# Seven plain value blocks in layer 0 of a four-layer kernel, and attention outputs repacked through DRAM from 512 to 448 rows ahead of the output projection

## The chip, the cores and the metric

One core of a Trainium2 chip. The time is the device time of one execution in microseconds (us). The kernel before takes 396.25 us (median of 3, 396.03 to 396.76). Most executions agree within 1%. Profiles show one execution each, on the same core; their span starts at the first instruction and is some 1.7 us shorter than the timed run.

## The reference

Four layers, A, B, A, B, each `x = x + layer(layernorm(x))`, on 2048 tokens of width 448, bf16.

```python
def _A_ref(x, wqkv, wo):              # H = 16 heads of 28, window W = 8, dilation 2
    q, k, v = ...                     # x @ wqkv, split by head
    idx = pos[:, None] - arange(W) * 2          # each token sees itself and 7 earlier ones, 2 apart
    logits = einsum("bhsd,bhswd->bhsw", q, kg) * 28 ** -0.5   # masked where idx < 0
    o = einsum("bhsw,bhswd->bhsd", softmax(logits), vg)
    return o.reshape(B, S, D) @ wo
def _B_ref(x, w_gate, w_up, w_down):  # F = 1792
    return ((x @ w_gate) * (x @ w_up)) @ w_down
```

## The kernel before

The program states operations with estimated durations, dependencies and priorities; a list scheduler in the program turns them into one fixed order for each engine, and semaphores carry the dependencies. All is unrolled. Tokens go through attention in value blocks of 120 queries; most attention operations serve a pair of blocks. The output projection works on double blocks of 256 tokens, 8 of them in each of the layers 0 and 2.

A head has 28 values; it sits in 32 rows, so that four heads fill the 128 partitions. The normalised attention `oT` is therefore 4 x 128 = 512 rows, 64 of which are padding, and the projection reads it as it stands, 8 chunks of 64 rows against weights with zeros in the padding:

```python
oT = sb([128, 4, HALF], bf, "oT")
...  # normalisation, VectorE, key ("N", li, qb)
tensor_tensor(oT[:, :, a % HALF:...], O, R_sb, ALU.mult)
...
def y_blocks(li, B, prio):
    twin_blocks(lambda w: ps[:, bk[w], 0:D],
                lambda w, c, lo: oT[lo:lo + 64, c, 128 * ((B + w) % 8):...],
                lambda w, c, lo: wo_g[lo:lo + 64, c, :], ..., [range(4)], ..., nd + WO, prio, bk)
```

For values, twelve heads are multiplied out by TensorE (336 columns). The last four ride in the padding rows of the query/key weights and reach their place over DRAM (`vt`), by 7 stores per chunk and a transposed load per block. The first three blocks of layer 0 (`PLAIN = 3`) skip that and multiply out all 448 columns. Loads and stores are issued by the Sync engine (SP) in the program's fixed order; what stands ahead holds up what is ready (4.3 us for the stores of one double block in the changed kernel's trace, below).

## Time and profile before

| | before |
|---|---|
| time | 396.25 us |
| TensorE (PE) busy | 98% of the span |
| PE in the chain that ended last | 88% |
| PE waiting, from 57.8 to 376 us | 2.3 us |

The prediction below shows the page's main lines. Two more things matter for what follows. The waits of PE (line waited for, total us, times, longest), the longest and the one at the end:

```profile
PE ps L877 <- issue: 1.8, 1, 1.8
...
PE ps L985 <- DVE hT L973: 0.9, 1, 0.9
```

The whole list has six entries, and no DMA is among them. "issue" means that PE stood still with nothing in the profile to wait for. And two stretches that the prediction left out (columns: stretch, length, busy time of PE, weight loads, VectorE, ScalarE, GpSimd, then PE clock, DMA share, GB/s):

```profile
57.80:143.00 85.20, 85.00 (x1398) 47.98 (x1398) 70.03 (x155) 45.28 (x92) 0.00 (x0) 1.00 0.29 48
143.00:245.00 102.00, 101.69 (x1664) 57.06 (x1662) 75.37 (x161) 49.92 (x97) 0.00 (x0) 1.00 0.22 37
```

PE loses 0.2 us in the first and 0.3 us in the second.

### The profile page before, as it was taken

How to read it: one execution, taken by the hardware profiler on the slowest of the kernel's cores; microseconds unless marked ns; L12 is line 12 of the kernel's file. 1: busy time of each engine (PE TensorE's matmuls, PEld its weight loads, DVE VectorE, ACT ScalarE, POOL GpSimd, SP SyncE). 2: the span in 40 equal slices, each digit the busy share in tenths (PEclk: the TensorE clock that was granted, in tenths of full speed). 3: DMA queues.
4: the chain of work that ended last, by engine and by line, in shares of the span. 5: the costliest groups of instructions: out<-in, count | busy, mean ns of one | idle time of the engine just before them, and what ended most of it. 6: DMA issues, size and time to landing. Idle time of an engine off the chain costs nothing.

```text
span 396.3 us, 13913 instructions
## 1 busy us (share of the span) xinstructions
PE 386.9 (98%) x6142; PEld 217.3 (55%) x6142; DVE 279.8 (71%) x604; ACT 199.4 (50%) x387; POOL 10.0 (3%) x38
## 2 busy tenths in 40 slices
PE   8999999999999999999999999899999999999996
PEld 5645468555445455545556677554545444544584
DVE  6997899988957857785679656695693867344152
ACT  5779895647514556345643445653661354043040
POOL 7200000000000000000000000000000000000000
PEclk9999999999999999999999999899999999999999
DMA  8992153532021412031020354008002120400000
GB/s 270 289 285 60 26 67 62 61 75 53 2 49 28 75 17 54 7 54 20 11 49 3 54 76 73 3 8 124 20 2 48 58 40 0 79 18 2 24 27 23
DMA packets 54107, 22.71 MB, mean 57 GB/s; under 512 B 44992, under 2 KB 53120, under 8 KB 54048
## 3 DMA queue, kind: packets, MB, share of 16 engines
q1 hardware_dynamic: 53136, 19.72, 25.4%
q10 hardware_dynamic: 912, 2.12, 1.9%
q8 instruction: 48, 0.79, 0.9%
q14 instruction: 11, 0.09, 0.1%
HBM read 8.54 MB, written 2.83 MB: 29 GB/s over the span
## 4 chain that ended last, share of the span: by engine, by line
PE 88%; DVE 6%; ACT 2%; issue 2%; DMA 1%; DVEq 0%
PE ps L964 42%; PE ps L698 25%; PE ps L682 15%; PE ps L877 2%; PE ps L843 2%; PE ps L985 1%; DVE st L614 1%; DVE x_sb L935 1%; DVE xn_sb L635 1%; DMA x_sb<-in_A_x_dram 1%; DVE E_sb L860 1%; PE ps L644 1%; DVE qk L734 1%; ACT qk L734 0%; DVE R_sb L905 0%
## 5 line engine op out<-in xcount | busy, mean ns | idle before, releaser
L964 PE MATMUL ps<-xnTb,WGU 64*128 64x512 bf16 (+1 forms) x1960 | 181.3, 336 | 0.6 <-ACT qk L734 0.4
L964 PEld LDWEIGHTS ps<-xnTb,WGU 64*128 64x128 bf16 x1960 | 95.1, 95 | 73.2 <-DVE x_sb L935 0.7
L970 ACT ACTIVATE g_sb<-ps 128x512 bf16<-128x512 f32 (+1 forms) x140 | 71.4, 513 | 121.7 <-PE ps L964 120.4
L973 DVE TENSOR_TENSOR hT<-g_sb,ps 128x512 bf16<-128x512 bf16 (+1 forms) x140 | 78.8, 573 | 42.3 <-ACT g_sb L970 38.8
L698 PE MATMUL ps<-WD,hT 64*128 64x448 bf16 x840 | 83.3, 349 | 0.0
L698 PEld LDWEIGHTS ps<-WD,hT 64*128 64x128 bf16 x840 | 40.7, 94 | 37.4
L935 DVE TENSOR_TENSOR x_sb<-x_sb,ps 128x448 bf16<-128x448 bf16 x62 | 35.9, 613 | 30.5 <-PE ps L698 30.4
L682 PE MATMUL ps<-xnTa,WQK 64*128 64x512 bf16 (+1 forms) x504 | 53.7, 353 | 0.6 <-DVE qk L734 0.2
L850 ACT ACTIVATE E_sb<-ps 128x1024 bf16<-128x1024 f32 (+1 forms) x36 | 33.9, 984 | 14.0 <-PE ps L843 13.0
L614 DVE BATCH_NORM_STATS2 st<-x_sb 128x6 f32<-128x448 bf16 x64 | 37.3, 614 | 2.7 <-DMA x_sb<-in_A_x_dram 2.7
L682 PEld LDWEIGHTS ps<-xnTa,WQK 64*128 64x128 bf16 x504 | 23.8, 94 | 22.8 <-DVE v_sb L823 0.6
L635 DVE TENSOR_SCALAR xn_sb<-x_sb,mv,rstd 128x512 bf16<-128x512 bf16 (+1 forms) x64 | 34.4, 585 | 0.8 <-ACT rstd L619 0.8
L734 ACT ACTIVATE qk<-ps 128x1024 bf16<-128x1024 f32 (+1 forms) x26 | 22.9, 896 | 14.8 <-PE ps L682 14.6
L698 PE MATMUL ps<-wo_g,oT 64*128 64x448 bf16 x256 | 29.4, 349 | 0.1
L860 DVE TENSOR_TENSOR E_sb<-E_sb,MK 128x1024 bf16<-128x1024 bf16 (+2 forms) x39 | 23.3, 610 | 6.2 <-ACT E_sb L850 6.1
L918 DVE TENSOR_TENSOR oT<-O_sb,R_sb 128x480 bf16<-128x480 f32 (+3 forms) x36 | 22.0, 624 | 5.6 <-ACT R_sb L907 5.2
L905 DVE STREAM_SHUFFLE R_sb<-O_sb 128x480 f32<-128x480 f32 (+1 forms) x34 | 22.5, 697 | 0.0
L682 PE MATMUL ps<-WV,xnTa 64*128 64x336 bf16 (+3 forms) x252 | 21.1, 299 | 0.5 <-DVE qk L734 0.2
L906 ACT ACTIVATE R_sb<-R_sb 128x480 f32<-128x480 f32 (+1 forms) x34 | 19.9, 602 | 1.9 <-DVE R_sb L905 1.9
L617 ACT ACTIVATE lnv<-mv,eps_sb 128x2 f32<-128x2 f32 (+1 forms) x33 | 9.4, 294 | 22.4 <-DVE mv L616 22.2
L907 ACT ACTIVATE R_sb<-R_sb 128x480 f32<-128x480 f32 (+1 forms) x34 | 19.9, 603 | 0.3
L698 PEld LDWEIGHTS ps<-wo_g,oT 64*128 64x128 bf16 x256 | 12.4, 94 | 11.7 <-PE ps L698 0.5
(50 smaller groups left out, 183.8 us busy)
## 6 DMA issues: line engine op xcount, KB each, us to landing
out_dram<-x_sb SPq DMA_DIRECT2D x15, 112.0 KB, 1.7
WD<-in_B_w_down_dram SPq DMA_DIRECT2D x2, 784.0 KB, 10.7
x_sb<-in_A_x_dram SPq DMA_DIRECT2D x3, 448.0 KB, 6.1
WGU<-in_B_w_up_dram SPq DMA_DIRECT2D x1, 896.0 KB, 18.2
WGU<-in_B_w_gate_dram ACTq DMA_DIRECT2D x1, 896.0 KB, 16.9
vt<-qk SPq DMA_DIRECT2D x49, 16.0 KB
WGU<-in_B_w_up_dram SPq DMA_DIRECT2D x1, 672.0 KB, 17.0
WGU<-in_B_w_gate_dram ACTq DMA_DIRECT2D x1, 672.0 KB, 12.3
```

The source lines that it names most:

```text
L614: sc.add("dve", one(lambda E, B=B: E.bn_stats(st6[:, B, :], x_sb[:, B, :]), ("bn", li, B)), 525.0, deps=[("x", li - 1, B)] + ([("xn", li - ...
L635: sc.add("dve", one(lambda E, B=B, dst=dst, src=src: E.tensor_scalar(dst, src, mv[:, B, 0:1], rstd[:, B:B + 1], ALU.subtract, ALU.mult), ( ...
L682: parts[0 if s < 3 else 1][1].append((lambda E, w=w, c=c, lo=lo, st=st, sp_=sp_: E.matmul(u["out"](w), u["lhs"](w, c, lo, lo + 64), u["rhs ...
L698: ins.append((lambda E, w=w, c=c, lo=lo, st=st, sp_=sp_: E.matmul(outs(w), lhs(w, c, lo), rhs(w, c, lo), start=st, stop=sp_), keys[w] if s ...
L734: return E.activation(dst, src, ACT.Copy) if hasattr(E, "activation") else E.tensor_copy(dst, src)
L850: return E.activation(E_sb[:, slot, 2 * hp:2 * hp + 2, 0:w], ps[:, b0:b0 + 2, 0:w], ACT.Exp, scale=SCALE)
L860: return E.tensor_tensor(e, e, m, ALU.mult)
L905: sc.add("dve", one(lambda E: E.stream_shuffle(R_sb[:, rs, 0:w], O_sb[:, os_, 0:w], [DH] * 32), ("Rs", li, qb)), dve_est(w) + 100.0, deps= ...
L935: sc.add("dve", one(lambda E: E.tensor_tensor(x_sb[:, B, :], x_sb[:, B, :], ps[:, bk[w], 0:D], ALU.add), ("x", li, B)), dve_est(D), deps=[ ...
L964: ins.append((lambda E, u=u, k=k, w=w: E.matmul(u["out"](w), WGU[64 * w:64 * w + 64, k, 128 * u["fc"]:128 * u["fc"] + 128], X[64 * w:64 * ...
L970: sc.add("act", one(lambda E, gs=gs, bk=bk: E.activation(g_sb[:, gs, 0:nt], ps[:, bk[0], 0:nt], ACT.Copy), ("G", li, j, fc)), act_est(nt), ...
L973: sc.add("dve", one(lambda E, gs=gs, bk=bk, fc=fc: E.tensor_tensor(hT[:, fc, hs, 0:nt], g_sb[:, gs, 0:nt], ps[:, bk[1], 0:nt], ALU.mult), ...
```

## The change

The intent is to shorten PE, which is the bound. The normalised attention goes, still padded, to a ring `oS`; four stores per double block write it to DRAM without the padding, and three loads bring it back as 448 dense rows (`oL`, `oP`). The projection then needs 14 matmuls and not 16 per double block. Seven blocks of layer 0 get plain values and not three, which drops 7 stores and 4 transposed loads at the start. The scheduler's priorities, seed and estimates were tuned afresh. Its estimate of a PE group also got a term for the fetch of instructions in long groups of small matmuls (`FETCH`, `CREDIT`, not in the cut below); DMA traffic beside them does not enter it. The core of the diff, cut:

```diff
-PLAIN = 3
+PAIR_PLAIN = (7, 7)
+OW = 512
+ODL = 2100.0        # estimate: stores of a repack, last issue to landing
+OIL = 2000.0        # the same for its loads
-PR = {...}  JP = {...}  SEED = 375  JITTER = 0
+PR = {...}  JP = {...}  SEED = 279  JITTER = 0.5     # all other values
...
-    oT = sb([128, 4, HALF], bf, "oT")
+    oS = sb([128, 4, OW], bf, "oS")
+    oL = sb([128, 3, OW], bf, "oL")
+    oP = sb([128, OW // 256, 128], bf, "oP")
...
+        for b in range(4):
+            dst = o_dram[li].rearrange("(c b e) n -> b e c n", c=4, b=4)[b][:, :, t0:t0 + 256]
+            src = oS[32 * b:32 * b + DH, :, m0:m0 + 256]
+            sc.add("sp", ... dma_start(dst, src) ..., deps=nd, dma=f"d_o{p}", lat=ODL)
+        loads = [(oL[:, :, m0:m0 + 256], o_dram[li][0:384, t0:t0 + 256]...)]
+        loads += [(oP[64 * h:64 * h + 64, sl, :], o_dram[li][384:448, ...]) for h in range(2)]
+            sc.add("sp", ... dma_start(dst, src) ..., deps=[("OD", li, p)] + war, dma=f"d_i{p}", lat=OIL)
+        for flip in (0, 1):
+            for c in range(4 - flip):
+                    lhs = oL[...] if c < 3 else oP[lo:lo + 64, sl, :]
+                    ... E.matmul(ps[:, bk[w], 0:D], lhs, wo_g[lo:lo + 64, c, :], ...)
```

## The prediction

> **What bounds the kernel now.** I read the page first (busy shares and the chain that ended last), then a table of stretches, then the TensorE (PE) timeline in the stretches that stood out.
>
> ```profile
> PE 386.9 (98%) x6142; PEld 217.3 (55%) x6142; DVE 279.8 (71%) x604; ACT 199.4 (50%) x387; POOL 10.0 (3%) x38
> ...
> PE 88%; DVE 6%; ACT 2%; issue 2%; DMA 1%; DVEq 0%
> ...
> L698 PE MATMUL ps<-wo_g,oT 64*128 64x448 bf16 x256 | 29.4, 349 | 0.1
> ```
>
> PE is busy 98% of the span and is 88% of the chain; the next engine, VectorE, has 29% to spare. The output projection (third line) waited 0.1 us in all. So the kernel is one queue of matmuls, and a change pays what it takes out of that queue, plus idle time that it removes, minus idle time that it makes. The stretches (columns: length, then busy time of PE, weight loads, DVE, ACT, POOL, then PE clock, DMA share, GB/s):
>
> ```profile
> 0.00:10.80 10.80, 8.76 (x56) 6.35 (x57) 7.06 (x16) 5.71 (x12) 7.67 (x31) 1.00 0.87 279
> 10.80:57.80 47.00, 45.17 (x1028) 26.25 (x1029) 40.99 (x104) 40.29 (x79) 2.36 (x7) 1.00 0.62 145
> ...
> 245.00:258.00 13.00, 11.24 (x248) 7.69 (x244) 8.22 (x24) 8.13 (x18) 0.00 (x0) 0.87 0.17 23
> 258.00:376.00 118.00, 118.00 (x1518) 58.20 (x1516) 69.68 (x129) 44.74 (x79) 0.00 (x0) 1.00 0.18 34
> 376.00:396.30 20.30, 17.00 (x248) 13.71 (x242) 8.45 (x19) 5.38 (x14) 0.00 (x0) 1.00 0.10 30
> ```
>
> From 258 to 376 us PE is never idle. Time that is not plain work lies at the start, in the layer 0 attention (10.8 to 57.8, where DVE and ACT are nearly as full as PE), at 245 to 258 (clock 0.87) and in the tail. The third:
>
> ```profile
> 245.63 1.31 PE L877 MATMUL ps<-E_sb,v_sb 64*32 64x64 bf16 x123
> 248.71 0.21 PE L877 MATMUL ps<-E_sb,v_sb 64*32 64x64 bf16 x5 [1.76 <-issue]
> 248.85 4.13 PE L964 MATMUL ps<-xnTb,WGU 64*128 64x256 bf16 x42
> 252.82 0.81 PE L682 MATMUL ps<-xnTa,WQK 64*128 64x512 bf16 x6
> ```
>
> Two attention-times-value groups (128 small matmuls) ran back to back; PE stopped for 1.76 us with no semaphore to wait for, and the next 42 matmuls took 3.97 us start to start, where such matmuls take 2.3 elsewhere. The clock record shows 0.5 for 3.41 us there. The packets of the instruction queue start at 240.8, 246.3 and 249.8 us: the stall sits over such a fetch. In all this cost some 3.6 us.
>
> [...]512 columns at 1.51 us for 7 pairs is 215.8 ns a pair[...]. The trace's instruction queue moved 48 packets of 16 KiB for about 12,400 PE instructions[...]; here a group before a score group is about 93 ns longer. [...]112 KB stores land here in 1.7 us.
>
> **The change part by part.** Prices are PE starts to the next group's start (two 64-row matmuls run side by side, so 8 matmuls are 4 pairs):
>
> ```profile
> 103.84 0.92 PE L698 MATMUL ps<-wo_g,oT 64*128 64x448 bf16 x8
> 104.60 1.67 PE L964 MATMUL ps<-xnTb,WGU 64*128 64x512 bf16 x14
> 106.11 0.92 PE L698 MATMUL ps<-wo_g,oT 64*128 64x448 bf16 x8
> ...
> 178.21 2.16 PE L682 MATMUL ps<-WV,xnTa 64*128 64x336 bf16 x28
> 180.20 3.19 PE L964 MATMUL ps<-xnTb,WGU 64*128 64x512 bf16 x28
> 183.32 0.71 PE L843 MATMUL ps<-qk 28*64 28x64 bf16 x64
> ```
>
> (1) Projection. Before, 512 rows (16 heads padded to 32) are 8 chunks of 64, 16 matmuls per two blocks of tokens; packed to 448 rows there are 14. One pair costs (104.60 - 103.84) / 4 = 0.19 us; 8 double blocks x 2 layers x 0.19 = 3.0 us less. (2) Plain value blocks, 7 in place of 3: blocks 3 to 6 of layer 0 are computed with all 448 columns, not 336. A 336 pair costs 1.99 / 14 = 0.142 us, a 448 pair 0.189; 14 pairs x 0.047 = 0.65 us more. In return 7 stores to DRAM and 4 transposed loads go, and the query/key matmuls of chunk 1 no longer wait for the patched weights. (3) Order. The built program has 83 changes of tiling kind on PE against 74; with about 0.1 us for a pair of changes, 0.45 us more. Sum of plain PE work: -3.0 + 0.65 + 0.45 = -1.9 us.
>
> (4) The repack: 4 stores and 3 loads per double block, 112 DMAs more, all issued by the Sync engine, at about 0.35 us each (7 stores took 2.43 us to issue in one row of that queue), 39 us of a queue that mostly waits. Latency: 4 x 0.35 + 1.7 and 3 x 0.35 + 1.7 is about 6 us between the normalised attention and its projection. Before, 6.7 us went from the start of an attention-value group (323.09) to its projection (329.76); so 12.5 us will be wanted. Pricing the new PE order as above, the tightest distance in it is some 13.6 us, the widest 17. So in a quiet stretch nothing waits. In layer 0, where transposed loads landed after up to 5 us in place of 3, some projections will be late. I allow 0.5 us.
>
> (5) The stall at 245 us. The new order has two back-to-back pairs of value groups in place of three. The three took 1.61, 3.23 and 1.33 us, and only one had the clock drop. I take 1.5 us as the expected loss of the new two, with more DMA beside the fetch, against 3.6 us: -2.1.
>
> (6) The end. Before, the last blocks wait for the last products:
>
> ```profile
> 388.42 5.50 PE L985 MATMUL ps<-WD,hT 128*128 128x448 bf16 x42 [0.93 <-DVE hT L973]
> ```
>
> In the new order, the previous chunk's down projection (98 of 112 matmuls) comes after them, so this 0.93 us is filled; but the program now ends with two full 448-wide additions (0.61 each) and a 112 KB store, in place of one 224-wide addition (0.39): about 0.7 us more. Net -0.25.
>
> (7) The head: same loads, one DVE memset of 0.8 us less, transposes in another order. Above the plain prices layer 0 lost 4.3 us between 10.8 and 75 us, with VectorE and ScalarE full. I see no lever that halves it, and projections now hang on two more DMA hops in the stretch with the most traffic. I allow +0.2.
>
> Sum: -1.9 + 0.5 - 2.1 - 0.25 + 0.2 = -3.55 us, or 392.7 of 396.25. The order of the new program was evidently tuned afresh (every priority differs), which tends to find a little more than I can see: I say 392.3.
>
> **The rivals.** First, that the repack's latency becomes the bound: each of 16 projections late by 1 us, and with the Sync queue in order, everything behind them late too. Against it: 13.6 us of distance for 12.5; for it: the margin is thin and 56 of the added DMAs fall in layer 0. That would give back 4 to 8 us: 396 to 400. Second, that the fetch stall does not go but comes elsewhere, perhaps twice: the two remaining pairs of groups, beside more DMA. Then 395 to 398. Third, that the new order also fills layer 0, so that only start, tail and 373 - 1.9 us of plain work stay: 371.2 + 10.3 + 3.2 + about 3 gives 387.7. For it: one wait on patched weights is gone; against it: VectorE and ScalarE stand at 87% there and their work is the same. Fourth, that only the projection counts (3 us saved, nothing else moves): 393.9 with the values' 0.65.
>
> **Range and chances.** The sure part is 2 to 2.4 us of columns; the stall swings by 3.6 and waits in layer 0 by some 3 either way. So 389.0 to 396.5 should hold it 8 times in 10. Over 2% faster means under 388.3, which needs the third rival: 0.09. Over 2% slower means above 404.2, which needs the first one at its worst: 0.02. Within 2%: 0.89.
>
> **What would show it.** Projection matmuls 224 in place of 256, with idle before them still near 0.1 us (step 4 right) or a few us with the repacked tile's load named as releaser (rival one). Value matmuls with 448 columns 42 in place of 14. Clock 1.00 in every stretch after the start and no idle "issue" of over 1 us in a value group (step 5). A tail of about 3.2 us from the last matmul's start. The prediction fails if projections wait, if the clock drops again, or if layer 0 ends more than 3 us earlier or later against its plain work.

## The result

The changed kernel is correct and takes 409.72 us (median of 4, 409.42 to 414.32), beside 396.14 us for the one before in the same rounds. The ratio is 1.037 (95% interval 1.030 to 1.045): slower. One further execution, in the slow state (over 1.5% above the fastest), took 420.41 us and is not counted. Ratios here are the mean time of one kernel's fast runs over that of the other's in the same rounds, so they are not quite the ratio of the medians quoted. The prediction, 392.3 with a range up to 396.5 and 0.02 for "slower by over 2%", was wrong.

The page of the changed kernel (the slowest of those four executions, 414.3 us), with the lines that answer to the three at the head of the prediction:

```profile
PE 387.9 (94%) x6110; PEld 212.9 (52%) x6110; DVE 275.5 (67%) x606; ACT 202.9 (49%) x392; POOL 7.3 (2%) x35
...
PE 67%; DMA 11%; SPq 7%; DVE 7%; ACT 4%; issue 3%; DVEq 0%
...
L972 PE MATMUL ps<-wo_g,oL 64*128 64x448 bf16 x192 | 24.1, 358 | 12.7 <-DMA oL<-o 7.9
```

PE does the same amount of work (387.9 us against 386.9, with part of it at half clock), but in a span 16 us longer. The chain has changed its nature: DMA and the Sync queue, 1% before, are 18% of it. The projection group now shows 12.7 us of idle time ahead of it where it had 0.1; the other 32 of its 224 matmuls read `oP` and stand in a row of their own. The waits of PE in this execution:

```profile
PE ps L972 <- DMA oL<-o: 7.9, 4, 3.4
PE ps L866 <- issue: 3.9, 1, 3.9
PE ps L972 <- DMA oP<-o: 2.8, 4, 1.4
```

Two things are new: 10.7 us of waiting for repacked rows, and one stop of 3.9 us that waits for nothing. A further 1.9 us before a projection is put down to VectorE by the profile (`R_sb`, double block 1), but that block's rows landed at 65.33 us and PE went on at 65.37, so some 12.6 us in all are waits for the repack. The stretches say where:

```profile
10.80:57.80 47.00, 42.31 (x902) 23.03 (x904) 34.33 (x87) 34.06 (x62) 0.88 (x4) 0.93 0.54 142
57.80:143.00 85.20, 74.87 (x1330) 40.91 (x1328) 66.71 (x154) 45.23 (x94) 0.00 (x0) 0.98 0.37 77
...
245.00:258.00 13.00, 13.00 (x172) 8.13 (x168) 5.57 (x14) 4.54 (x10) 0.00 (x0) 1.00 0.39 77
258.00:376.00 118.00, 115.25 (x1732) 57.96 (x1728) 79.15 (x155) 55.14 (x98) 0.00 (x0) 1.00 0.26 57
```

Ten of the microseconds are lost between 57.8 and 143 us, where the loss before was 0.2; 2.75 between 258 and 376; and in the head (10.8 to 57.8) PE is idle for 4.7 us rather than 1.8, and runs at a mean clock of 0.93. At 245 to 258 us the stop that the prediction hoped to remove is indeed absent.

**The repack.** From the trace, for each double block, the time from the end of its normalisation to the landing of its last load (us):

```text
layer 0, double blocks 0-7:   9.0 11.3 10.6 13.6  6.6 11.2  7.6  6.3
layer 2, double blocks 8-15:  8.4  7.4  7.0  8.3  8.4  9.7  8.3 10.3     mean 9.0
PE idle ahead of its projection: block 1 2.0, 2 1.4, 3 2.8, 5 3.4, 8 0.8, 12 0.6, 14 0.9, 15 0.6
```

Double block 3 shows why. It was normalised at 73.55 us. The Sync queue (start, time of issuing, instruction), then PE:

```profile
73.90 1.19 SPq L774 DMA_TRANSPOSE v_sb<-vt  x1
75.15 2.62 SPq L658 DMA_TRANSPOSE xnTb<-xn_sb  x2
77.82 2.22 SPq L958 DMA_DIRECT2D o<-oS  x4
80.10 2.40 SPq L774 DMA_TRANSPOSE v_sb<-vt  x2
82.61 1.81 SPq L964 DMA_DIRECT2D oP<-o  x2
84.45 0.60 SPq L964 DMA_DIRECT2D oL<-o  x1
```

```profile
87.17 0.74 PE L972 MATMUL ps<-wo_g,oL 64*128 64x448 bf16 x6 [2.79 <-DMA oL<-o]
```

Three transposed loads, 1.2 to 1.3 us each to issue, stand ahead of the stores, which so start 4.3 us after the rows are ready; then the stores take 2.2 us to issue, and two more transposes stand ahead of the loads. The rows landed at 87.12 us. The Sync queue waited 13.4 us in ten places (the longest 3.1) for stores of the repack to land, and issued nothing else in that time.

**The stop.** The PE timeline of the changed kernel at its place (start, length, group, idle time before):

```profile
28.25 0.30 PE L866 MATMUL ps<-qk 28*64 28x72 bf16 x24
32.45 0.28 PE L866 MATMUL ps<-qk 28*64 28x72 bf16 x8 [3.90 <-issue]
32.67 3.17 PE L702 MATMUL ps<-xnTa,WQK 64*128 64x512 bf16 x14
```

A score group of 32 matmuls is cut after the 24th. The 14 matmuls after it take 3.10 us to the next group's start, where they take 1.61 at full clock: the clock record has 0.5 for 6.83 us here.

### The profile page after: what moved, and what is told of

The parts are those of the page before. It is cut to its first block, busy times and chain, and to the rows that moved or that the text cites. A ratio compares the mean times of both kernels' runs of the same rounds, so it can differ in the third digit from the quotient of the medians.

```text
span 412.6 us, 13955 instructions
## 1 busy us (share of the span) xinstructions
PE 387.9 (94%) x6110; PEld 212.9 (52%) x6110; DVE 275.5 (67%) x606; ACT 202.9 (49%) x392; POOL 7.3 (2%) x35
## 4 chain that ended last, share of the span: by engine, by line
PE 67%; DMA 11%; SPq 7%; DVE 7%; ACT 4%; issue 3%; DVEq 0%
PE ps L1010 29%; PE ps L718 16%; PE ps L702 13%; PE ps L972 5%; DMA oL<-o 3%; DMA oP<-o 3%; DMA o<-oS 3%; SPq L964 3%; SPq L958 2%; PE ps L900 2%; DVE xn_sb L655 2%; PE ps L1031 1%; PE ps L866 1%; DMA hT<-in_A_wqkv_dram 1%; DMA xnTa<-xn_sb 1%
## 5 line engine op out<-in xcount | busy, mean ns | idle before, releaser
L1010 PE MATMUL ps<-xnTb,WGU 64*128 64x512 bf16 (+1 forms) x1960 | 178.9, 334 | 0.7 <-ACT g_sb L1016 0.5
L702 PE MATMUL ps<-xnTa,WQK 64*128 64x512 bf16 (+1 forms) x504 | 56.7, 365 | 1.0 <-DMA xnTa<-xn_sb 0.4
L972 PE MATMUL ps<-wo_g,oL 64*128 64x448 bf16 x192 | 24.1, 358 | 12.7 <-DMA oL<-o 7.9
L942 DVE TENSOR_TENSOR oS<-O_sb,R_sb 128x480 bf16<-128x480 f32 (+7 forms) x40 | 22.2, 577 | 4.1 <-ACT R_sb L930 3.8
L972 PEld LDWEIGHTS ps<-wo_g,oL 64*128 64x128 bf16 x192 | 8.2, 95 | 23.5 <-DMA oL<-o 12.0
```

The source lines that it names most:

```text
L702: parts[0 if s < 3 else 1][1].append((lambda E, w=w, c=c, lo=lo, st=st, sp_=sp_: E.matmul(u["out"](w), u["lhs"](w, c, lo, lo + 64), u["rhs ...
L972: ins.append((lambda E, w=w, c=c, lo=lo, lhs=lhs, flip=flip: E.matmul(ps[:, bk[w], 0:D], lhs, wo_g[lo:lo + 64, c, :], start=c == 0 and fli ...
L1010: ins.append((lambda E, u=u, k=k, w=w: E.matmul(u["out"](w), WGU[64 * w:64 * w + 64, k, 128 * u["fc"]:128 * u["fc"] + 128], X[64 * w:64 * ...
```

## The experiments

Fifteen kernels ran. "Same order" means that the changed kernel's order on every engine was kept and only what is named was altered. The two causes suspected from the trace are the repack (waiting for it, or its traffic) and the stop with the half clock after it; the rival is the order itself, tuned for other durations. Times are medians of all executions, with the time of the kernel before of the same rounds behind the slash where it is not 396.68. The ratios leave out executions in the slow state (one of four in a_again, f2_wdlate and a_spread2, two of four in a_spread), so where the two differ, go by the ratio.

### The changed kernel again: a_again

> The changed kernel unaltered, to see what is usual in it. Theory W (the projections wait for the repacked attention output: in the first profile TensorE idled 12.7 us before them, and its clock was halved for 3.4 us after one of those stops) expects again 409 to 410 us and again 10 to 13 us idle before the projections. The stop of 3.9 us without a semaphore at 28 us, followed by 6.8 us at half clock, belongs to the slowest execution (414.3); if it is occasional, it is missing or shorter here, and the span is some 5 us shorter than 412.6. If it is part of the change's cost, it is here too.

408.28 us (405.58 to 412.95), ratio 1.027 (1.020 to 1.034). The profile fell on an execution of 406.0 us with the clock at 1.00 throughout:

```profile
PE ps L972 <- DMA oL<-o: 7.5, 4, 2.8
...
PE ps L866 <- issue: 1.7, 2, 1.1
```

With `oP`'s 2.7 us, which stand between these two lines, the 10 us for repacked rows are there in both executions looked at. The stop is not fixed: 1.7 us in two places here, 3.9 us and a half clock in the other profile. So the changed kernel's spread is partly the stop's.

### Not waiting, and not repacking: f1_nowait, f2_padded, g_free

Three kernels in the same order close a square. f1_nowait keeps the repack transfers, but the projection reads a constant tile (wrong result on purpose, relative error 1.01):

```diff
-lhs = oL[...] if c < 3 else oP[lo:lo + 64, sl, :]
+lhs = wo_g[lo:lo + 64, c, 128 * w:128 * w + 128]
+# projections no longer depend on the loads; the loads keep their own order
```

> Every engine's order as in the changed kernel and all 112 DMAs of the repack still run, but the projection reads a constant tile in place of the repacked one, so it waits for no repack (wrong result on purpose). Theory W expects 396 to 399 us: 409.6 less some 11 us of idle and some 2 us of half clock. Rival O (the new order of work is slow in itself, and the waits only stand where others would) expects 405 us or more. Rival D (the added DMA traffic slows instruction fetch and transposes) also expects 405 or more, as the traffic is still there.

f2_padded drops the 112 transfers and projects from the padded rows with 16 matmuls, as before (correct):

```diff
-oS, oL, oP; wo_g packed
+oT = sb([128, 4, HALF], bf, "oT"); wo_g padded, as in the kernel before
+mm(E, 1, 3, 0, 1); mm(E, 0, 3, 64, 1)     # the two matmuls more per double block
+sc.order["sp"] = [o for o in sc.order["sp"] if not a repack transfer]
```

> Every engine's order as in the changed kernel, but the repack taken out: the projection reads the padded 512 rows straight from SBUF with 16 matmuls per double block, and the 112 DMAs are gone. Right result. Theory W expects 397 to 401 us: no wait for DMA before the projections, and 16 x 0.19 = 3.0 us of matmuls more than the run without waits. Rival O expects 405 us or more. Rival D expects it clearly faster than the run without waits, by more than 2 us, as the traffic is gone.

g_free is f1_nowait without the 112 transfers (wrong on purpose): the change as if the repack were free.

> The changed kernel's order with 14 projection matmuls per double block that read a constant tile, and none of the 112 repack transfers (wrong result on purpose): the change as if the repack were free. Against f2_padded (400.8 us, 16 matmuls, no repack) only the 32 matmuls are gone: my price says -3.0 us, 397.8 us. If it is there, traffic of the repack costs 403.5 (f1_nowait) - 397.8 = 5.7 us and waiting for its rows 408 to 410 - 403.5 = 5 to 6 us. Rival: the packed projection gives less (399 us or more), because the shorter projection only moves waits; then the change had no 3 us to win at all.

| | matmuls | repack transfers | waits for them | time | ratio (95%) |
|---|---|---|---|---|---|
| a_again | 14 | yes | yes | 408.28 | 1.027 (1.020 to 1.034) |
| f1_nowait | 14 | yes | no | 403.48 | 1.018 (1.014 to 1.022) |
| g_free | 14 | no | no | 398.31 / 396.21 | 1.006 (1.003 to 1.008) |
| f2_padded | 16 | no | no | 400.83 | 1.010 (1.007 to 1.014) |

f2_padded came within theory W's 397 to 401 us; f1_nowait lies between the two figures named for it, and neither theory alone foresaw it. Waiting for the rows costs 408.28 - 403.48 = 4.8 us (409.72 would give 6.2), the transfers themselves 403.48 - 398.31 = 5.2 us, and the packed projection gains 400.83 - 398.31 = 2.5 us of the 3.0 priced. Taken from the ratios, which allow for the rounds, the three are 3.6, 4.8 and 1.7 us, each to within some 3.3, 1.8 and 1.7 us (estimates, from the two intervals that each is the difference of). How can transfers that nobody waits for cost 5 us? In f1_nowait other DMAs arrive late, behind them:

```profile
PE ps L1010 <- DMA xnTb<-xn_sb: 3.2, 1, 3.2
PE ps L900 <- DMA v_sb<-vt: 1.5, 1, 1.5
```

A transposed load of activations is 3.2 us late and one of values 1.5 us, neither of which is in the changed kernel's list of waits. These runs do not tell apart whether the transfers are in the way as traffic or as places in the Sync queue. The stop is in this kernel as well (3.7 us in two places), and in f2_padded too (2.8 us at the same place, and 6.83 us of half clock after it), where there is no repack at all. So it is a second, separate cost.

### The stop: f2_wdlate, s6_wdlate, d_quiet, e_spread

At 20 to 28 us the share of busy DMA is 1.05 and 1.04 in the two stretches of f2_padded: the weights of layer 1 are coming in. If the stop is an instruction fetch that has to stand behind them, moving these loads should move or remove it. f2_wdlate issues the down-projection weights some 30 us later, on top of f2_padded; s6_wdlate does the same to the changed kernel:

```diff
+wd = [o for o in sc.order["sp"] if o.dma in ("d_wd0", "d_wd1")]
+at = next(i for i, o in enumerate(rest) if o.dma == "d_p0_2")   # value stores of chunk 2
+sc.order["sp"] = rest[:at + 1] + wd + rest[at + 1:]
```

> The run without the repack (padded projection, same order), with the down-projection weights loaded later as in the other run. Theory F expects 394.5 to 396.5 us: 400.8 less the 2.8 us stop and some 2.7 us of half clock. Its rival expects 400 to 401 us.

402.29 us / 396.28 (ratio 1.015, 1.007 to 1.022). At 28 us the stop shrank from 2.8 to 1.2 us and no half clock followed it; but at 44 us, beside the moved load (DMA share 0.89 from 42 to 46), a new one of 2.7 us came, with 3.4 us of half clock. Moved, not removed, and slower than either theory's figure.

> The changed kernel in the same order on every engine, except that the two loads of the down-projection weights (1.5 MB) are issued some 25 us later, after the first store of chunk 2's value rows. Theory F (the stop at 28 us is an instruction fetch that queues behind the weight loads, which keep all DMA engines full until about 31 us; the new order runs more small matmuls there) expects no idle time over 0.5 us without a semaphore at 26 to 33 us, a clock of 1.00 there, and 403 to 406 us. Rival (the stop comes from the number of small matmuls alone) expects it still there, 2 to 4 us, and 408 us. The waits before the projections stay (some 10 us) in both.

418.91 us / 396.28 (ratio 1.056). A clear miss: with the repack in place the moved load met it. The waits for repacked rows rose to 14.8 us (11.2 and 3.6), and the DMA share from 46 to 50 us was 1.03. Nor did the stop at 28 us go: 2.3 us of it were left, with no half clock after it. So the late load was made smaller instead. d_quiet asks for the down-projection weights at 52 us and for the second halves of the gate and up weights after the first score group (29 us), on top of f2_padded:

> The padded projection in the changed kernel's order (f2_padded, 400.8 us), with the down-projection weights asked for only after the last early value stores (about 56 us) and the second halves of the gate and up weights only after the first score group (about 29 us), so that the DMA rings are less full while the instruction queue fetches at 28 us. Theory F (the stop at 28 us and the half clock after it come from instruction fetches that stand behind bulk weight loads): no stop of TensorE named issue above 0.5 us up to 60 us, clock 1.00 from 10 to 60 us, 395 to 397.5 us. Rival M (stops follow wherever the bulk load goes): a new stop of 1 to 4 us at 55 to 65 us, 400 to 403 us. Rival O (the order itself is what is slower): no stop, clock 1.00, and still 399 us or more.

398.08 us / 396.01 (ratio 1.0042, 1.0024 to 1.0059), clock 1.00 to the end of the work. The stop at 28 us is gone, and two came at 40 and 44 us:

```profile
PE ps L701 <- issue: 1.6, 1, 1.6
...
PE ps L865 <- issue: 1.1, 1, 1.1
```

The time lies between what theories F and O named. e_spread also cuts the second halves of those weights into four pairs of loads of 224 KB, asked for after four successive attention groups:

```diff
+gates = [k[-1] for o in peo for _, k in o.ins if attention group of layer 0][1:5]
+for n, k in enumerate(range(3, 7)):
+    for nm, lo, wsrc in (("wu", 64, B_w_up), ("wg", 0, B_w_gate)):
+        plain_dma("sp", WGU[lo:lo + 64, k, :], wsrc[64 * k:64 * k + 64, :], ..., deps=[gates[n]])
```

> d_quiet (398.1 us) with the second halves of the gate and up weights cut in four transfers each and asked for in four pairs, after four successive attention groups between 29 and 35 us[...]. Theory F/M (a fetch stands behind whatever bulk load is under way): the stops at 40 and 44 us (2.7 us in all) shrink below 1 us and the time falls to 395.5 to 397 us, level with before. Rival (the stops come from the density of small matmuls, whatever the load): the stops stay and the time stays at 397.5 to 399 us.

396.67 us / 396.21 (22 runs, ratio 1.0010, 0.9992 to 1.0027): level with before. One stop of 1.0 us is left. f2_padded and e_spread at the place of the stop:

```profile
28.34 0.30 PE L865 MATMUL ps<-qk 28*64 28x72 bf16 x24
31.49 0.29 PE L865 MATMUL ps<-qk 28*64 28x72 bf16 x8 [2.84 <-issue]
```

```profile
28.29 0.34 PE L866 MATMUL ps<-qk 28*64 28x72 bf16 x32
```

And the DMA share ahead of that place, f2_padded first, then e_spread (the number before the last in the line):

```profile
24.00:28.00 4.00, 3.77 (x104) 2.44 (x102) 2.80 (x9) 3.74 (x8) 0.88 (x4) 1.00 1.04 302
```

```profile
24.00:28.00 4.00, 3.77 (x104) 2.44 (x102) 2.80 (x9) 3.74 (x9) 0.88 (x4) 1.00 0.01 2
```

The same 104 matmuls in the same order, and DMA full in one and empty in the other. Three more facts from the traces bear on what the stop is.

Its place: the instruction queue moved 48 packets of 16 KiB in before and in the changed kernel, for 12,423 and 12,357 instructions of PE (matmuls, weight loads, and nearly all of the rest semaphore waits), one packet for 259 and 257 of them. Counted from the start in blocks of 256, the stops named here come after number 193 or 194 of a block, in every kernel: at 28 us in the changed kernel, f1_nowait, f2_padded, g_free and f2_wdlate, at 40 and 44 us in d_quiet, at 43 us in e_spread and, in the kernel before, at 248.7 us.

Its end: packets of 16 KiB of the instruction queue started at 16.9 and then only at 28.7 us in f2_padded, and PE went on at 31.5; in the changed kernel at 16.2 and 29.7, and PE went on at 32.45. In e_spread that packet started at 23.2 us, 5.5 us earlier than in f2_padded, and there was no stop at 28 us.

Why the kernel before has none: its packet is late as well (25.1 us, DMA share 1.02 and 1.03 from 20 to 28). But by the same count (from number 193 of one block to that of the next) PE entered this stretch of 256 at 21.3 us and left it at 28.3, 7.0 us later. In the changed kernel it begins at 23.9 and its last matmul before the stop starts at 28.4, after 4.5 us, because 88 of the 96 small matmuls of two score groups lie in it. That PE needs the packet at the end of the stretch, so that before had 7.0 us for the fetch and the new order 4.5, is the author's reading of these times. At this place the order alone makes no stop (e_spread), and full DMA alone makes none (before); both together do (2.84 us in f2_padded, 3.90 in the changed kernel).

Together the stops and their half clock are worth 400.83 - 396.67 = 4.2 us (3.6 by the ratios). The length of the stop did not decide whether the half clock came: it followed stops of 1.76 us (before, for 3.41 us) and 2.84 us (f2_padded, for 6.83 us), and did not follow one of 2.79 us (the changed kernel, at 87 us) or 2.29 us (s6_wdlate).

### Both at once: a_spread, a_spread2

Does the cure of e_spread help the changed kernel, repack included?

> The changed kernel, repack and all, with only the weight loads spread as in e_spread (down-projection weights at about 50 us, second halves of gate and up in four pairs of small transfers from 29 us). If the causes add up: 4 us less than the changed kernel's 408 to 410 us, so 404 to 406 us, no TensorE stop named issue above 1 us before 60 us, clock 1.00 there, and the waits for repacked rows still near 10 us. Rival: with 56 more transfers in the same stretch the moved loads meet the repack's stores and loads, the waits for repacked rows grow by 2 us or more or the stops stay, and the time is 407 us or more (as it was when the down-projection weights alone were moved, 418.9 us).

417.74 us / 395.88 (ratio 1.045, 1.035 to 1.055), a miss, and not a fair test: my eight loads stood in the Sync queue behind the first three stores of the first repacked double block and so went out together at 39.6 to 45 us, and the fourth store went out only 6.1 us after the third. It shows again what one transfer out of place does in a queue in order. a_spread2 puts them ahead of the first repack store and leaves the down-projection weights early:

> The changed kernel, repack and all, with only the second halves of the gate and up weights cut into four pairs of small loads, asked for after four attention groups from 29 us and all ahead of the first repack store in the Sync queue; the down-projection weights stay early. If the causes add up: the stop of 2 to 4 us at 28 us and the half clock after it shrink below 1 us, waits for repacked rows stay near 10 us, and the time is 404 to 406 us. Rival (the repack's transfers bring the stops or longer waits back): 407 us or more.

408.20 us / 396.55 (404.38 to 410.97; ratio 1.026, 1.015 to 1.037). The stop at 28 us is gone (one of 1.3 us at 43 us is left), and yet the time is that of a_again:

```profile
10.80:57.80 47.00, 44.87 (x1016) 25.47 (x1018) 39.45 (x102) 38.56 (x70) 0.88 (x4) 1.00 0.57 146
57.80:143.00 85.20, 75.34 (x1272) 40.86 (x1270) 65.77 (x150) 42.99 (x90) 0.00 (x0) 0.98 0.37 78
```

PE is busy 2.6 us longer in the head than in the changed kernel's first profile, at full clock, but no more than there between 57.8 and 143 us, and waits 12.1 us for repacked rows (9.2 and 2.9), where a_again's profile has 10.2 and the changed kernel's first some 12.6. The two costs may overlap, so that PE, where it comes earlier, waits longer; that is argued and not shown. The intervals (1.015 to 1.037 here, 1.020 to 1.034 in a_again) leave room for a gain of 4 us and for none; the fastest execution, at clock 0.999, took 404.4.

### More distance, other latencies, another queue: f4_shift1, s4_lat, f3_poolq

f4_shift1 moves every part of a projection one PE group later, in the changed kernel:

```diff
+for each projection part i, from the last to the first:
+    pe[i], pe[i + 1] = pe[i + 1], pe[i]
```

> The changed kernel with every projection part moved one TensorE group later (about 1 to 2 us more distance between the normalised attention and its projection), nothing else. Theory D (the repacked rows simply come some 1 to 3 us later than the order allows): waits of the projection for repacked rows fall from about 10 us to 4 to 6, and the time to 403 to 406 us against about 408 in the same rounds as before at 396.5. Rival S (the Sync engine's in-order queue or other waits set the pace, so that more distance is eaten at once): waits stay at 8 us or more, or come back under another name, and the time stays within 1.5 us of the changed kernel's 408 to 410.

415.33 us / 396.01 (ratio 1.050). The time is a miss for both theories. The waits for repacked rows fell as theory D said, to 1.7 us, but others came in their place:

```profile
PE ps L1010 <- DVE hT L1019: 4.2, 5, 1.3
PE ps L1010 <- DVE x_sb L980: 3.8, 4, 1.3
...
PE ps L972 <- DMA oP<-o: 1.3, 1, 1.3
```

In the second line gate/up groups wait for an addition to the residual; the likely reading, argued and not tested, is that they need the PSUM banks which a projection now frees later. More distance is to be had only by a new order of everything. s4_lat lets the scheduler make one, with honest latencies (stores 3.3 us and 0.44 an issue, loads 2.8 and 0.56):

> The changed kernel with only the scheduler's numbers for the repack raised: 0.44 us per store issue and 0.56 per load issue in place of 0.34, and 1.2 and 0.8 us more to landing, as the profile of the changed kernel shows; so it places the projections later. Theory W with the mis-sized distance expects idle before projections under 5 us and 400 to 405 us. Rival O expects 408 us or more, as a new order drawn from the same priorities gains nothing.

421.80 us (ratio 1.064), a miss. The waits for repacked rows did fall (3.9 us for `oP`, none for `oL` among the longer ones), but the new order has an 8.1 us wait for a transposed load and 4.1 us of stops. The priorities are tuned to one set of estimates; with others, they give an order that nobody tuned. f3_poolq takes the repack out of the Sync queue and has GpSimd issue it, in the same order:

> The changed kernel in the same order, but the 112 DMAs of the repack are issued by GpSimd, which is idle, and no longer stand in the Sync engine's queue between transposes that wait for VectorE. Theory H (a good part of the repack's delay is standing in line behind other entries of the in-order queue: in layer 0, 2.8 and 4.4 us between the normalised output and the first store) expects idle before projections to fall from 10 to 5 us or less, and 402 to 405 us. Rival L (the two DMA hops themselves, some 3 and 3 us, are the delay) expects 407 us or more; slower still if a DMA from GpSimd takes longer to issue.

417.33 us / 396.28 (ratio 1.055). A miss for the theory that standing in line is all: waits of 7.1 and 6.4 us, not less than 10. It is not a clean test, as all 112 stand in one queue there too, and from GpSimd the stores took 2.2 and the large loads 3.0 us to land (the loads 2.6 from Sync).

### The parts of the kernel before: b_split, b7_plain7

The prediction counted on 3.6 us to be had where two value groups follow each other at 245 us. b_split puts the next PE group between the two, in the kernel before:

```diff
+for i in range(len(pe) - 1, 0, -1):
+    if pe[i].mode == pe[i - 1].mode == "C32":
+        pe[i], pe[i + 1] = pe[i + 1], pe[i]
```

> The kernel before in the same order, except that in its three back-to-back pairs of attention-value groups one unit of gate and up matmuls is put between the two. If the stop of 1.8 us at 245 us and the half clock after it come from 128 small matmuls in a row outrunning the fetch of instructions, and if it is in most executions, it is gone here and the time is 392.5 to 394.5 us against 396.7; the clock is 1.00 all along. If it was an accident of one execution, the time stays within 1 us of before.

397.17 us / 396.28 (20 runs, ratio 1.0026, 1.0004 to 1.0048): no gain. There is no stop at 245 us in its profile and the clock is 1.00 throughout, and it isn't faster. The profile of before that the prediction read was that of a run of 398.05 us, where 396.3 is usual; its stop is not in the kernel's usual execution. It may not be unique either: of the 101 executions of before in these experiments, 25 have a granted clock under 0.999, mostly the 0.996 of that profile, and their mean is 398.0 us, where that of the other 76 is 395.9. They were not profiled, so where their clock was halved is not known.

b7_plain7 is the kernel before with seven plain blocks, rescheduled:

> The kernel before with seven plain value blocks in layer 0 and its own padded projection, rescheduled with its own priorities: the other half of the change alone. My price for it was +0.65 us of matmul columns, against four transposed loads and seven stores less: 396.5 to 398 us if the price is all that counts; up to 400 us if rescheduling with priorities tuned for three plain blocks costs as it did in s4_lat; below 395.5 us if the loads that it drops were a hidden cost in layer 0.

400.61 us / 396.01 (ratio 1.012, 1.007 to 1.018). More than the price, and inconclusive as to the plain blocks: the profile shows no large new wait (the longest are two of 1.2 us), but a new order with more small waits, as in s4_lat. What the plain blocks cost in a tuned order is bounded only together with the rest, by e_spread, which has them: 0.5 us for everything in that order.

By the author's account, of which the record has nothing, a kernel with the repack in layer 2 only deadlocked in simulation and was not run. None of the kernels beats the one before; e_spread equals it, with the projection as before.

## Why the prediction was wrong

The account, from the runs in the changed kernel's order, each against the next:

| term | from | us, medians | us, ratios |
|---|---|---|---|
| order, plain blocks, tail: all that is left | e_spread - before | +0.5 | +0.4 |
| stops and half clock | f2_padded - e_spread | +4.2 | +3.6 |
| 14 matmuls for 16 | g_free - f2_padded | -2.5 | -1.7 |
| traffic of the repack | f1_nowait - g_free | +5.2 | +4.8 |
| waiting for its rows | a_again - f1_nowait | +4.8 | +3.6 |
| sum | | +12.1 | +10.7 |

Each term is a run against the next, so the sum is a_again against before and must close; that it does is no proof of the parts. The ratio column, of fast executions alone, is the safer one; by the intervals its terms from the second on are good to some 1.5, 1.7, 1.8 and 3.3 us (estimates). The terms depend on the sequence in which they are taken, and a_spread2 could not show that the second is to be had while the repack is there. (One ratio point is taken as 3.96 us.)

Step 1 (projection, -3.0 us) was right in kind: -1.7 to -2.5, where the intervals do not exclude 3.0. It is the only gain.

Steps 2 and 3 (plain values +0.65, changes of kind +0.45) are not tested one by one: with the tail and all else they leave +0.5 in e_spread, which fits them, but no run separates them.

Step 4 (the repack) is the step that failed. "About 6 us between the normalised attention and its projection" was a sum of issue times and one landing time in a quiet queue. It measured 6.3 to 13.6, mean 9.0, because a store took 0.46 us to issue on average and a load 0.61, in single cases up to 1.9 (0.35 assumed), because the Sync queue had transposes ahead of both, and because it stood still for 13.4 us while it waited for the stores. The other half of the distance was wrong as well: 6.7 us from the start of a value group to its projection were taken from a quiet stretch, and for double block 3 it took 13.7 us (59.84 to 73.55) to the end of the normalisation alone. "I allow 0.5 us" should have been some 4 to 5 (3.6 by the ratios), and the effect on the other transfers, another 5, was not in the sum at all; the prediction saw that the queue "mostly waits", but not that what stands behind a wait in it is late too (in a_spread the fourth store went out 6.1 us after the third). This is the first rival, "the repack's latency becomes the bound: each of 16 projections late by 1 us, and with the Sync queue in order, everything behind them late too". Its mechanism was right, though not every projection was late but 8 of 16 in the first profile, by 0.6 to 3.4 us; it was priced at 4 to 8 us and given almost no chance to exceed that.

Step 5 (the stop at 245 us, -2.1) fell: there was nothing to gain there (b_split), as the kernel's usual time does not contain it. Its size was a little off too: 1.76 us of stop and 3.97 - 2.3 of slow matmuls are 3.4 us, not 3.6. The second rival, "the fetch stall does not go but comes elsewhere", was right in kind, but not in place: it came in the head, where step 7 allowed 0.2 us and it cost about 4. The reason could have been seen beforehand: the profile of before has the DMA share at 1.02 and 1.03 from 20 to 28 us, and the built order shows 88 of the 96 matmuls of two score groups in one stretch of 256 instructions there.

Step 6 (tail -0.25): the wait of 0.93 us is gone as foreseen, and the end from the last matmul's start grew from 2.65 to 3.64 us. Net near zero, right within some 0.3 us.

One landing was priced about right: the loads of the repack mostly landed 1.4 to 2.3 us after the end of their last issue (1.7 assumed). But the hop through DRAM has a store and a load in series, with the issuing queue held between, and 9.0 us was the mean.

## What to carry to other kernels

The hop through memory cost two landings here, and before each the time that its issue stood in line in a queue, 6.3 to 13.6 us in all; and other loads came late beside it (3.2 and 1.5 us in f1_nowait). Price such a hop from the busiest stretch of the trace, in the order that will be run, and compare that with the few microseconds which it saves. Dense groups of small matmuls beside bulk loads that fill the DMA engines (share 1.04) stopped PE here, for 2.8 us in f2_padded; cutting such loads into pieces of 224 KB, spread out in time, and asking for others later won 4 us in the kernel without the repack (e_spread), without touching the order of the matmuls. With the repack no gain could be shown. And before a stop in one profile is counted as time to be won, compare that execution's time with the usual one.
